# Loading the second batch's first rows between two weight blocks, with 12 stand-in matmuls instead of 16

## The chip, the core and the metric

The kernel runs on one core of one Trainium2 chip. The metric is device time in microseconds (us) of one execution; lower is better. The engines are PE (matmuls, with a separate weight-load track), DVE, ACT and POOL for elementwise work, and SP, which here only issues DMAs. ACT and POOL issue DMAs too.

## What is computed

A global filter along the sequence, then a two-layer network with SiLU on every token:

```python
batch, seq, dim = (8, 3008, 256)          # tokens 8 * 3008 = 24064, d_ff = 2048
X = np.fft.rfft(x, axis=1)
Y = X * (filt_r + 1j * filt_i)[None, :, :]
attn_out = np.fft.irfft(Y, n=x.shape[1], axis=1).astype(np.float32)

h = attn_out.reshape(B * S, D) @ w_in      # (24064, 256) @ (256, 2048)
g = h * (1.0 / (1.0 + np.exp(-h)))
out = (g @ w_out).astype(np.float32)       # (24064, 2048) @ (2048, 256)
```

The weights `w_in` and `w_out` arrive in double precision.

## The kernel before

**The main loop.** The network of all eight batches is a loop of 384 steps (`hidden`, `project`): 48 pairs of token blocks times 8 groups of hidden channels, all matmuls in fp32 (L756 and L819), a Strassen-like scheme with seven products per group. While it runs for batch b, the filter of batch b+1 is worked in between its rounds by a planner (`plan`, `put`), at step and round times written out by hand. That covers nearly all of the time. The instruction order of each engine is the program's order.

**The prologue** is what comes before the loop, some 74 us. It computes the filter of batch 0 alone, converts the first nine weight blocks, and begins batch 1:

- `weights(j)` (L1009, `load_weights` at L904) loads block j of the double-precision weights as two DMAs of 256 KB on SP: 128 columns of w_in (L926) and 128 rows of w_out (L929). Below, w5 stands for block 5, with a first and a second half. `bits`, `converted`, `rounded` and `placed` turn the two 32-bit words of each number into fp32 on DVE and ACT.
- `stage1_first` (L295) is the first transform of batch 0 on PE. It reads x from `w_t`, which is borrowed as a buffer, and from `x_all`.
- `load_filters` (L235) brings the filter on the queues of SP, ACT and POOL; `d_t` and `e_t` are tables of the transforms, loaded by ACT in two parts each (L1069, L1075; L1073, L1076).
- `table` (L1089) makes signed copies of `e_t`; for groups 2 to 5 on ACT (L1095).
- `forward` (L456), `products`, `inverse` (`inverse_first`, L516, and `rows_first`, L531) carry batch 0 through its six groups: matmuls pb (L467) and pc (L527), and between them the multiplication by the filter. `rows_first` copies the result q out of PSUM (L541) and stores it to DRAM (L543): ten of the twelve stores are issued by ACT, each directly behind its copy, and the second ones of groups 4 and 5 by SP.
- `load_t4_rows` (L567) reads those rows back, six DMAs of 256 KB on SP (L571) into a part of `w_t`.
- `second["load_two"]` (L326, through `load_rows`, L275) loads the rows that batch 1's first two stage-1 steps need: one DMA of 768 KB on SP (L277) into `x_all`, called x below. It may not start before `stage1_first` has read batch 0's rows out of `x_all`.
- `second["stage1"]` (L339, L345) transforms them: eight passes on PE. The copies out of PSUM follow on ACT (L361).
- `idle_wide(16)` (L1051, L1055) are stand-ins: matmuls whose result nobody reads, issued by PE between batch 1's stage 1 and the last stage of batch 0. Each is 128x256 and two passes.
- `stage3` (L574, pd, L586) is the last transform of batch 0, and reads the rows that `load_t4_rows` brought. Its copies to y (L600) release the main loop.

SP and ACT issue their DMAs in the program's order. In the prologue SP's order is: w0 to w3, x of batch 0, its share of the filter, a small table (`wi_t`, L1077), w4 to w7, x of batch 1, w8, the two stores of q, the six loads of rows, w9.

Of the kernel before, what the change touches and what calls it, by code (L numbers as in the profile page):

```python
# [170 lines left out]
def kernel(  # L171
# [79 lines left out]
    def bank(b, name, spare=None):  # L251


        if early[0] is None and spare in ("x", "yz"):
            return xps.tile([128, 2, C], FP32, name=name, tag=spare)
        if early[0] is None and spare is not None:
            return accps.tile([128, 2, C], FP32, name=name, tag=f"a{spare}")
        if early[0] is None:
            return fps.tile([128, 2, C], FP32, name=name, tag="f")
        early[0] += 1  # L260
        k = early[0] % 8
        if k < 2:
            return fps.tile([128, 2, C], FP32, name=name, tag="f")
        if k > 5:
            return xps.tile([128, 2, C], FP32, name=name, tag="x" if k == 6 else "yz")
        return accps.tile([128, 2, C], FP32, name=name, tag=f"a{k - 2}")
# [637 lines left out]
    def load_weights(j, queue=None):  # L904

        if j in (8, 11, 12, 13):
            pool, tag = (t4pool, "t4") if j in (11, 12) else (upool, "u")
            raw = pool.tile([128, 2, 512], U32, name=f"raw_{j}", tag=tag)
        else:

            if j in (0, 2):
                t = ypool.tile([128, 2, HALF], FP32, name=f"raw_{j}", tag="y")
                raws.setdefault("tiles", []).append(t)
                raws["at"] = t.rearrange("p a n -> p (a n)").bitcast(U32)[:, 0:2048]
                raws["y"] = raws["at"]
                raws.setdefault("first", raws["at"])
            elif j == 4:
                raws["at"] = spool.tile([128, 2048], U32, name=f"raw_{j}", tag="s")
            elif j == 6:
                raws["at"] = gpool.tile([128, 2048], U32, name=f"raw_{j}", tag="g")  # L920
            elif j in (9, 14):
                raws["at"] = raws["y"]
            at = 1024 * (j in (1, 3, 5, 7, 10, 15))
            raw = raws["at"][:, at:at + 1024].rearrange("p (w n) -> p w n", w=2)
        queue = queue or nc.sync
        queue.dma_start(  # L926
            out=raw[:, 0].rearrange("p (a n) -> p a n", a=2),
            in_=moe_w_in.bitcast(U32)[:, 256 * j:256 * j + 256].rearrange("(a p) n -> p a n", p=128))
        queue.dma_start(out=raw[:, 1], in_=moe_w_out.bitcast(U32)[128 * j:128 * j + 128, :])  # L929
        raws[j] = raw  # L930
# [78 lines left out]
    def weights(*js, queue=None):  # L1009
        for j in js:  # L1010
            if wide:
                load_weights(j, queue)
# [38 lines left out]
    def idle_wide(n, ps=None, rhs=None):  # L1051

        ps = ps or bank(0, "idle")
        for _ in range(n):
            nc.tensor.matmul(out=ps[:, 0], lhsT=wx_t, rhs=wide_rows if rhs is None else rhs,  # L1055
                             start=True, stop=True)
# [18 lines left out]
    nc.scalar.dma_start(out=d_t[:, 16:NS], in_=d_dram[:, 16:NS])  # L1075
    nc.scalar.dma_start(out=e_t[:, 2:NG], in_=e_dram[:, 2:NG])  # L1076
    nc.sync.dma_start(out=wi_t, in_=ws_dram.ap())  # L1077
    weights(4, 5, 6, 7)

    signed = []  # L1080
    for i in range(2):
        t = typool.tile([128, 2, 2, 2, 128], FP32, name=f"signed_{i}", tag="ty")
# [26 lines left out]
    for k in range(16):  # L1109
        part["stage1_first"](k, 2)  # L1110
        if k in whole:
            part["stage1_first"](whole[k], 3)
    second["load_two"]()
    weights(8)
    part["forward"](0, fill=4)
    placed(0, 1)
    for g in range(1, 4):
# [49 lines left out]
    gp.tensor_copy(out=gate, in_=w_t[:, 4, A11, 0, 0:1])  # L1167
    for u in range(2):
        second["store_rows"](u)
    idle_wide(16)  # L1170
    for g in range(4):
        part["stage3"](g)
    nc.sync.dma_start(out=wi_t, in_=wi_dram.ap())
# [93 lines left out]
```

## Time and profile before

Four runs gave 2574.99, 2577.04, 2577.07 and 2578.72 us: median 2577.06. The execution that the profiler recorded took 2574.76 us.

| what | value |
|---|---|
| profiled execution, device time | 2574.76 us |
| its span in the profile | 2572.9 us, 47850 instructions |
| PE busy | 2551.3 us (99%) |
| weight loads (PEld) busy | 2195.7 us (85%) |
| DVE / ACT / POOL busy | 1664.9 / 1091.8 / 430.7 us |
| mean granted clock of PE | 0.996 |
| mean DMA rate | 66 GB/s; 300 and 151 GB/s in the first two of 40 slices |

The span is cut into 40 slices of 64 us for the overview; the prologue is the first slice and a part of the second. There the DMA engines are busy at 90% or more in the first slice and 50% in the second, and in the second slice the granted PE clock is at 0.8 of full speed. In all other slices the clock is at 0.9 or more, and PE is busy for 80% to over 90% of the time.

How the lines are read: a timeline line has its start, its duration, the engine (SPq and ACTq are DMA issues), the line in the kernel, the operation, output<-inputs, and how many are merged; in square brackets stands the engine's idle time ahead of it and what ended that. A matmul in fp32 is recorded as two passes. A DMA in the chain of waits lasts from its issue to its landing.

### The profile page before, as it was taken

To read this page: it belongs to the slowest core of one execution; us is meant where nothing else is said; L and a number is where in the kernel's file an instruction comes from. 1 tells how busy PE (TensorE), PEld (TensorE's weight loads), DVE (VectorE), ACT (ScalarE), POOL (GpSimd) and SP (SyncE) were. 2 spreads that over 40 slices of the span, in tenths; PEclk is the share of its full clock that TensorE was granted. 3 is DMA by queue.
4 is the path that set the end of the run, shared out by engine and by line. 5 is a ranking of instruction groups with operands and counts; after the bars stand their busy time and mean duration, and the time that the engine had idled before them with its cause. 6 is when DMAs were issued, how large, how long until landed. Compare 5 with 4: busy or idle time off the path is not lost.

```text
span 2572.9 us, 47850 instructions
## 1 busy us (share of the span) xinstructions
PE 2551.3 (99%) x18714; PEld 2195.7 (85%) x18714; DVE 1664.9 (65%) x3589; ACT 1091.8 (42%) x3019; POOL 430.7 (17%) x688
## 2 busy tenths in 40 slices
PE   8999999999999999999999999999999999999998
PEld 6688888888888888888888888888888888888987
DVE  7866666676666666666666676666666666555554
ACT  4544444444444444443444344444444444444443
POOL 4212111211121111211121112211121112101101
PEclk9899999999999999999999999999999999999999
DMA  9522232222222222322233122331232211200011
GB/s 300 151 60 55 74 73 64 60 74 66 58 66 66 73 69 48 82 71 66 58 74 77 48 67 63 76 79 46 66 87 66 66 42 33 60 17 16 9 17 16
DMA packets 198554, 171.06 MB, mean 66 GB/s; under 512 B 122068, under 2 KB 173380, under 8 KB 197348
## 3 DMA queue, kind: packets, MB, share of 16 engines
q1 hardware_dynamic: 176056, 117.06, 19.7%
q0 software_dynamic: 17344, 45.70, 5.6%
q10 hardware_dynamic: 4928, 5.24, 0.7%
q8 instruction: 147, 2.41, 0.4%
q14 instruction: 79, 0.65, 0.1%
HBM read 96.07 MB, written 81.26 MB: 69 GB/s over the span
## 4 chain that ended last, share of the span: by engine, by line
PE 96%; DMA 3%; DVE 1%; ACT 0%; issue 0%; ACTq 0%; SPq 0%; DVEq 0%
PE acc L819 44%; PE px L756 26%; PE pyz L756 19%; PE pd L586 3%; PE pb L467 2%; PE pc L510 2%; PE pf L434 1%; DMA w_t<-in_x_dram 0%; PE pa L354 0%; DMA raw<-in_moe_w_out_dram 0%; DMA x_all<-in_x_dram 0%; DMA d<-q 0%; PE pa L345 0%; DMA filt<-in_filt_i_dram 0%; DMA d_t<-d_tbl 0%; DMA w_t<-d 0%
## 5 line engine op out<-in xcount | busy, mean ns | idle before, releaser
L819 PE MATMUL acc<-g,w_t 128*128 128x256 f32 (+1 forms) x5376 | 1508.8, 375 | 0.4 <-DVE g L727 0.4
L819 PEld LDWEIGHTS acc<-g,w_t 128*128 128x128 f32 x5376 | 1021.3, 190 | 115.6 <-DVE g L727 0.8
L727 DVE TENSOR_TENSOR g<-pyz,abc 128x256 f32<-128x256 f32 (+1 forms) x1152 | 480.0, 417 | 619.8 <-ACT abc L777 356.2
L727 DVE TENSOR_TENSOR g<-g 128x256 f32<-128x256 f32 (+3 forms) x1152 | 599.6, 520 | 196.8 <-ACT g L760 183.7
L756 PE MATMUL px<-ty,w_t 128*128 128x256 f32 (+1 forms) x2304 | 678.5, 376 | 1.1 <-ACT abc L771 0.6
L760 ACT ACTIVATE g<-g 128x256 f32<-128x256 f32 (+1 forms) x1152 | 472.9, 410 | 250.2 <-DVE g L727 250.2
L727 POOL TENSOR_TENSOR s<-s 128x256 f32<-128x256 f32 (+1 forms) x329 | 255.2, 793 | 1417.3 <-DVE s L839 1320.8
L756 PEld LDWEIGHTS px<-ty,w_t 128*128 128x128 f32 x2304 | 432.1, 190 | 65.4 <-issue 6.0
L756 PE MATMUL pyz<-y,w_t 128*128 128x256 f32 (+1 forms) x1536 | 453.6, 377 | 0.5 <-DVE g L727 0.4
L756 PEld LDWEIGHTS pyz<-y,w_t 128*128 128x128 f32 x1536 | 283.5, 189 | 48.0 <-DVE g L727 7.9
L771 ACT COPY abc<-px 128x256 f32<-128x256 f32 (+1 forms) x384 | 141.5, 369 | 372.3 <-PE px L756 372.3
L777 ACT COPY abc<-px 128x256 f32<-128x256 f32 (+1 forms) x384 | 141.8, 369 | 338.2 <-PE px L756 337.4
L760 ACT ACTIVATE g<-px 128x256 f32<-128x256 f32 (+1 forms) x384 | 146.1, 380 | 300.0 <-PE px L756 299.9
L756 PE MATMUL px<-y,w_t 128*128 128x256 f32 (+1 forms) x768 | 232.2, 384 | 0.8 <-DVE y L600 0.8
L756 PE MATMUL pyz<-ty,w_t 128*128 128x256 f32 (+1 forms) x768 | 225.8, 376 | 0.3 <-DVE g L727 0.2
L756 PEld LDWEIGHTS px<-y,w_t 128*128 128x128 f32 x768 | 140.3, 189 | 32.7 <-DVE y L606 5.8
L756 PEld LDWEIGHTS pyz<-ty,w_t 128*128 128x128 f32 x768 | 144.6, 190 | 19.1 <-DVE g L727 1.5
L764 ACT COPY abc<-px 128x256 f32<-128x256 f32 (+1 forms) x384 | 135.8, 354 | 52.2 <-PE px L756 52.2
L586 PEld LDWEIGHTS pd<-wi_t,t 48*64 48x64 f32 x3840 | 61.1, 135 | 25.1 <-ACT g L760 16.4
L446 POOL DMA_DIRECT2D d<-tf x144 | 71.9, 506 | 28.8 <-DVE tf L442 28.8
L839 ACT COPY s<-acc 128x512 f32<-128x512 f32 (+1 forms) x94 | 54.3, 578 | 47.5 <-PE acc L819 47.4
L869 DVE STREAM_TRANSPOSE o<-s 128x256 f32<-128x256 f32 x192 | 73.9, 423 | 0.4 <-issue 0.4
(136 smaller groups left out, 1270.7 us busy)
## 6 DMA issues: line engine op xcount, KB each, us to landing
t<-d SPq DMA_DIRECT2D x120, 192.0 KB
t<-d SPq DMA_DIRECT2D x84, 256.0 KB
d<-q POOLq DMA_DIRECT2D x84, 256.0 KB, 2.7
out_dram<-o SPq DMA_DIRECT2D x636, 32.0 KB
d<-tf POOLq DMA_DIRECT2D x144, 96.0 KB, 3.3
xr<-in_x_dram SPq DMA_DIRECT2D x6, 1472.0 KB
x_all<-in_x_dram SPq DMA_DIRECT2D x72, 96.0 KB
x_all<-xr SPq DMA_DIRECT2D x72, 96.0 KB
```

The lines of the kernel that those rows point to most:

```text
L446: nc.gpsimd.dma_start(out=d1[k // 2, :, k % 2, n0:n0 + 4], in_=us["tf"][32 * k:32 * k + NS].rearrange("p q n c -> p (q n) c"))
L467: nc.tensor.matmul(out=ps[k][32 * j:32 * j + 32, ri, :], lhsT=d_t[rows, 4 * g + at, ri, :], rhs=rhs, start=True, stop=True)
L586: nc.tensor.matmul(out=ps[h][c0:c0 + 64, cb, i, :], lhsT=t4[rows, i, 128 * cb + c0:128 * cb + c0 + 64], rhs=wi_t[rows, :], start=True, sto ...
L727: eng.tensor_tensor(out=out, in0=in0, in1=in1, op=op)
L756: nc.tensor.matmul(out=out, lhsT=w_t[:, jp, c, 0], rhs=rhs, start=start, stop=True, skip_group_check=True)
L760: nc.scalar.activation(out=g[:, k, 0:n], in_=g[:, k, 0:n] if src is None else src, func=AFT.Silu)
L764: nc.scalar.copy(out=sums[:, 0, 0:n], in_=xo)
L771: nc.scalar.copy(out=sums[:, 1, 0:n], in_=xo)
L777: nc.scalar.copy(out=sums[:, 2, 0:n], in_=xo)
L819: nc.tensor.matmul(out=acc[pair][i][:, h, 0:n], lhsT=w_t[:, jp, c, 1], rhs=g[:, k, 0:n], start=(jp == 0 and h == 0), stop=last, skip_group ...
L839: copy(out=s[:, 2 * i:2 * i + 2, 0:n], in_=acc[pair][i][:, :, 0:n])
L869: v.transpose(out=o[:, :, h, :], in_=results[pair][:, ((2, 6), (4, 1))[chunk][h], :])
```

## The change

The loads of w5, w6 and w7 are issued behind x of batch 1 instead of ahead of it, and twelve stand-ins run instead of sixteen. The call for w4 moves to just ahead of x in the text.

```diff
@@ -1075,8 +1075,6 @@
     nc.scalar.dma_start(out=d_t[:, 16:NS], in_=d_dram[:, 16:NS])
     nc.scalar.dma_start(out=e_t[:, 2:NG], in_=e_dram[:, 2:NG])
     nc.sync.dma_start(out=wi_t, in_=ws_dram.ap())
-    weights(4, 5, 6, 7)
-
     signed = []
     for i in range(2):
         t = typool.tile([128, 2, 2, 2, 128], FP32, name=f"signed_{i}", tag="ty")
@@ -1110,8 +1108,9 @@
         part["stage1_first"](k, 2)
         if k in whole:
             part["stage1_first"](whole[k], 3)
+    weights(4)
     second["load_two"]()
-    weights(8)
+    weights(5, 6, 7, 8)
     part["forward"](0, fill=4)
     placed(0, 1)
     for g in range(1, 4):
@@ -1167,7 +1166,7 @@
     gp.tensor_copy(out=gate, in_=w_t[:, 4, A11, 0, 0:1])
     for u in range(2):
         second["store_rows"](u)
-    idle_wide(16)
+    idle_wide(12)
     for g in range(4):
         part["stage3"](g)
     nc.sync.dma_start(out=wi_t, in_=wi_dram.ap())
```

## The prediction, made before the changed kernel was run

> **What bounds the kernel now.** I read the engine totals first: PE is busy for 2551.3 of 2572.9 us and the chain of waits is 96% PE. The main loop is matmuls end to end and the change touches none of it. What can move is the stretch ahead of the loop, so I read the chain of waits there. Its columns are start, duration, what ran or was in flight.
>
> ```profile
> 32.94 8.69 DMA raw<-in_moe_w_out_dram
> ...
> 41.71 8.40 DMA x_all<-in_x_dram
> ...
> 50.18 0.37 ACTq L543
> 50.55 0.04 issue
> 50.59 0.60 ACT q L541
> ...
> 51.21 3.61 DMA d<-q
> ...
> 55.54 4.08 DMA d<-q
> ...
> 60.22 6.18 DMA w_t<-d
> 66.41 0.14 issue
> 66.54 7.12 PE pd L586 x254
> ```
>
> The chain says that x of the second batch (41.71) left when weight block 4's second half landed (32.94 + 8.69 = 41.63), and that ACT's sixth store of q (50.18) left when x landed (50.11). Neither needs the other's data. Counting the DMAs that SP and ACT issue, in the order of their issues, x is the eighth after w4's second half, and that store is the eighth after x. So each of these DMAs waits for the one eight places ahead. I use that rule below. From the last store of q (55.54) the chain runs through the load of its rows into w_t to stage 3 (pd) at 66.54.
>
> Then PE's own timeline, and the busy time and clock in five stretches (columns: busy us of PE, weight loads, DVE, ACT, POOL, then granted clock, DMA share, GB/s):
>
> ```profile
> 52.97 3.70 PE L345 MATMUL pa<-x_all,wx_t 96*128 96x512 f32 x8
> 56.50 7.07 PE L1055 MATMUL idle<-d_t,wx_t 96*128 96x256 f32 x32
> 65.56 0.41 PE L586 MATMUL pd<-wi_t,w_t 48*64 48x47 f32 x2 [1.99 <-DMA w_t<-d]
> 66.54 7.07 PE L586 MATMUL pd<-wi_t,w_t 48*64 48x47 f32 x254 [0.56 <-DMA w_t<-d]
> ```
>
> ```profile
> 63.60:65.10 1.50, 0.00 (x0) 0.00 (x0) 1.50 (x3) 1.50 (x4) 0.00 (x0) 1.00 0.71 171
> 65.20:66.50 1.30, 0.41 (x2) 0.28 (x2) 1.26 (x4) 1.27 (x3) 0.00 (x0) 0.50 1.05 255
> 66.60:73.60 7.00, 7.00 (x254) 6.85 (x254) 3.32 (x8) 2.17 (x6) 3.71 (x8) 0.50 0.29 70
> 74.40:78.80 4.40, 3.84 (x8) 2.15 (x8) 3.71 (x10) 1.84 (x5) 0.00 (x0) 0.50 0.85 225
> ```
>
> Three things: the second batch's stage 1 (L345) starts as soon as the matmuls before it are through, with x long landed; the stand-ins (L1055) end at 63.57 and PE then waits 1.99 us for DMA; and the clock is at half from before pd starts until 78.8, although 16 stand-ins ran. Last, the DMA queues (packets, MB, share) in 36 to 40 us, then in 44 to 48 us; q1 is SP's, q10 ACT's:
>
> ```profile
> q10 hardware_dynamic: 274, 0.74, 55.4%
> q1 hardware_dynamic: 630, 0.64, 48.2%
> ...
> q1 hardware_dynamic: 368, 0.98, 102.6%
> ```
>
> **The change, part by part.** **Four stand-ins fewer.** The 32 passes start every 0.216 us (56.5 to 63.2 for 31 intervals), so eight fewer take 8 x 0.216 = 1.73 us less. They end at 61.84 instead of 63.57. What hides this is the wait for w_t<-d: pd's first pass waits until 65.56 whichever number ran. Value 0. A gain of 1.73 us is excluded, since nothing waits for the last stand-in. A loss is possible only by the clock, and in this execution pd ran at half clock anyway, so nothing is left to lose: 0. If some executions keep the full clock through pd now, they would lose the difference: pd's 256 passes took 7.12 us here and 4 x 1.08 = 4.32 in the main loop (64 passes each, at 152.40 and 163.18 in the chain), that is 2.8 us. The upper end is +2.8.
>
> The Trainium skill, "TensorE: Matmul & The Clock Gate", section "Why this matters for your kernels", speaks against this edit: it wants no PE idle gap of more than about 3 us between bursts, or the clock falls back to half. By that rule the gap of 1.99 us should have kept the clock and the new one of 3.7 us would lose it, and the sum would be about 3 us worse; the row has the clock at half after 1.99 us already, and the row decides.
>
> **x moved ahead of w5 to w7.** w4's two DMAs only move in the text: no DMA stands between their old and their new place on SP, so they still leave at 31.07 and 32.94. x takes the place of w5's first half and leaves at 36.72, not 41.71. Its own data wait, for the first batch's stage-1 matmuls that read x_all, was over at 30.7. The six DMAs of w5 to w7 move back by one place: to 37.14, 37.65, 38.13, 40.02, 40.44 and 41.71. w8's first half stays at 42.09. w8's second half now has x eight places ahead and leaves when x lands. The bytes in front of ACT's stores of q are the same 2.8 MB, in another order.
>
> When does x land? In 36 to 40 us SP's queue moved 0.64 MB, of which 0.52 are w4 (512 KB), so what stands behind w4 begins near 39.6 (0.12 MB at some 300 GB/s). x's 768 KB at the 244 GB/s of 44 to 48 us, where x went, take 3.2 us: 42.8, and some 1.5 us to the landing (w4's packets were through near 40, its landing is 41.63): 44.3. w8's second half leaves 1.7 us later than now.
>
> Who is better off: ACT's sixth store. The stores before it come every 1.03 us (46.87, 47.90, 48.92); it should leave at 49.95 and left at 50.18. w7's second half is now eight ahead and stands behind the same bytes as x did, so it lands no later. Gain 0 to 0.23; ACT's chain is what the later pd steps wait for, so I take 0.23.
>
> Who is worse off: e_t's second part (512 KB, ACT's queue, 32.19), which ACT's tables wait for until 41.37; everything after hangs on them. Its last packets went in 36 to 40 us beside SP's, so x may cut in at the very end. Bounds: 0, and +0.6 (one packet of x for each engine: 96 packets over 16 engines in 3.2 us is 0.53 each). Value 0, because x begins when e_t is nearly through.
>
> Behind that stands the queue of stores: the last one took 4.08 us to land, the same stores from POOL 2.7 in the page's DMA list. If the queue empties earlier, up to 1.4 us come out of the chain at 55.54; if w8's late half mixes with the stores, up to +1.0 (one store's spacing). Between -1.4 and +1.0 I take 0: the bytes are the same.
>
> DVE reads w5 at 50.28, w6 and w7 from 55.43, w8 at 56.76; with w4's landing time, 8.69 us, the latest of them, w8's second half, is there at 53.0. These stay hidden, by 3.8 us at least. Without that cover, DVE's conversion would stall by what it is late, and then the `gate` copy on POOL with the stores of t1 behind it. x itself has 8.7 us to spare before 52.97.
>
> **Sum:** 0 - 0.23 + 0 + 0 = -0.2 us against the profiled execution's 2574.76 us (span 2572.9 and 1.9 around it). That execution lies 2.3 below the median of the runs, 2577.06; so the forecast is **2576.8 us, no change**. Its own range: -1.4 below, +0.6 + 1.0 above, and about 1.5 to each side for the spread of the runs (2574.99 to 2578.72): 2574 to 2580. The +2.8 of the clock, alone, ends inside it at 2579.6.
>
> **Rivals.** **A, slower: the wait goes from x to w8's second half.** ACT's eighth store (52.23) now stands behind it, where the queue is in order. It decides if that half lands after 52.0. For it: it leaves late, and 44.3 + 8.69 = 53.0 would already cost 1.0. Against: at 44.3 nothing but w7 and w8 is left in front of it, and the bytes are those that have landed by 52 today. If x lands no earlier than now (50.1; the engines sharing their time over all that is queued), w8's half comes at 50.1 + 3.6 (a store's latency) to 50.1 + 8.69, 53.7 to 58.8, and all of ACT's later stores, and pd, shift by 1.7 to 6.8 us: middle about +4, 2581.
>
> **B, faster: the rows for pd come early enough that the clock is held.** If the store queue drains early (-1.4, -0.23) and pd ran at full clock (-2.8) with the loop's first pairs (1.19 + 0.87 us in the chain, against 0.70 + 0.43 later, -0.9), the sum is -5.3: 2571.8. For it: each piece is a row. Against: PE's gap would still be 65.56 - 1.6 - 61.84 = 2.1 us, no shorter than the one after which the clock fell.
>
> **C, hidden altogether:** x was never waited for by PE, so moving it does nothing, not even 0.23: 2577.1. It isn't told from the forecast by time and shares its chance. That x can't go early, because of its data wait, is excluded by 30.7 against 36.72.
>
> **How the numbers follow.** Forecast with C 0.62, A 0.24, B 0.14. A difference of 0.2%, 5.2 us, is about what a measurement of this kernel can tell from no change. Of A some 0.17 lies beyond it, for what its far end may hold that I can't price (DVE waiting for w8 as well), of B 0.13. So faster 0.13, same 0.62 + 0.07 + 0.01 = 0.70, slower 0.17. The range takes in B's price and most of A: 2571.5 to 2582, leaving out about 0.1 at each end.
>
> **What would show it.** Right: x issued near 36.7; ACT's sixth store near 49.95; stand-ins through 1.7 us sooner and PE idle that much longer ahead of pd; pd near 66.3, at half clock. Wrong: ACT's eighth store waiting for w8 (A); pd's 256 passes in 4.3 us, or starting before 65 (B); ACT's tables starting after 42, which would be e_t pushed back. A difference that begins only in the main loop would refute all of it.

## The result, and the profile after

The changed kernel takes 2581.2 us (median of 35 executions, 2578.07 to 2584.22) against 2577.16 us of the kernel before (53 executions, 2574.33 to 2580.29). The ratio is 1.0016, 95% interval 1.0011 to 1.0021: **slower by 4.0 us, 0.16%**. The forecast was 2576.8 us, 4.4 below; the result lies at the upper end of its range, 2582. By the bound of 0.2% that the prediction took for a measurable difference this would still be no change, but over so many executions the interval excludes 1, and there is a small loss that the forecast had not. The profiled execution took 2580.88 us with a span of 2579.0; beside the one of before that is 6.1 us more.

Where the 6.1 us of this pair lie: the second acc matmul (L819), the end of the prologue, starts at 87.70 us instead of 82.33 (5.4 us), and from there to the 5001st acc matmul it is 2326.16 us instead of 2325.39 (0.8 us). The chain of waits of the changed kernel (start, us, what) no longer goes through x or through ACT's sixth store:

```profile
27.17 6.84 DMA filt<-in_filt_i_dram
...
47.99 10.32 PE pc L527 x64
58.31 1.93 PE pa L345 x4
...
64.07 7.71 DMA w_t<-d
...
71.91 7.12 PE pd L586 x254
```

PE itself is now in it, for 10.32 us of pc. PE's timeline of the same execution says why:

```profile
42.70 1.64 PE L467 MATMUL pb<-w_t,d_t 64*32 64x256 f32 x32
47.99 6.65 PE L527 MATMUL pc<-w_t,signed 64*128 64x256 f32 x31 [3.65 <-POOL z L497]
...
58.24 3.70 PE L345 MATMUL pa<-x_all,wx_t 96*128 96x512 f32 x8
61.78 5.34 PE L1055 MATMUL idle<-d_t,wx_t 96*128 96x256 f32 x24
70.84 0.42 PE L586 MATMUL pd<-wi_t,w_t 48*64 48x47 f32 x2 [3.72 <-DMA w_t<-d]
71.91 7.07 PE L586 MATMUL pd<-wi_t,w_t 48*64 48x47 f32 x254 [0.65 <-DMA w_t<-d]
```

PE stands still for 3.65 us ahead of 47.99 and then needs 6.65 us for 31 passes. In the kernel before it waited 0.28 us there, and 29 passes took 3.50:

```profile
45.87 3.50 PE L527 MATMUL pc<-w_t,signed 64*128 64x256 f32 x29 [0.28 <-ACT q L541]
```

Stage 1 (L345) starts at 58.24 instead of 52.97, the stand-ins are through in 5.34 us instead of 7.07, and the wait ahead of pd is 3.72 us instead of 1.99. The releaser named for the first gap, POOL's z, is not one: that matmul reads w_t and not z. What ended just before is ACT's first copy of q (47.28 + 0.56), which frees a PSUM bank: the kernel takes its eight banks in turn, and these matmuls, of group 2, get the ones that group 0 had. ACT's timeline, first of the changed kernel, then of the kernel before:

```profile
44.44 0.42 ACT L1093 ACTIVATE signed<-e_t 128x256 f32<-128x256 f32 x1 [27.28 <-DMA raw<-in_moe_w_out_dram]
...
47.28 0.56 ACT L541 COPY q<-pc 128x512 f32<-128x512 f32 x1
47.87 0.38 ACTq L543 DMA_DIRECT2D d<-q  x1
```

```profile
41.37 0.42 ACT L1095 ACTIVATE signed<-e_t 128x256 f32<-128x256 f32 x1 [23.30 <-DMA raw<-in_moe_w_out_dram]
...
44.80 0.38 ACTq L543 DMA_DIRECT2D d<-q  x1
```

The tables that ACT makes from e_t (L1095, now L1093) start 3.07 us later, and the first copy and store with them. The packets in the trace show e_t: its second part's 4 KB packets ran from 37.44 to 40.71 us before and run from 37.30 to 43.81 now, while x's 8 KB packets, once at 43.65 to 49.25, run at 37.98 to 43.32, beside them. The DMA queues from 36 to 40 us (packets, MB, share; q1 is SP's, q10 ACT's) say the same in the changed kernel; before, q10 had moved 0.74 MB there:

```profile
q1 hardware_dynamic: 485, 0.98, 79.0%
q10 hardware_dynamic: 109, 0.42, 30.9%
```

Last the granted clock (columns as in the prediction), three stretches of the changed kernel, then one of the kernel before:

```profile
44.00:48.00 4.00, 0.35 (x15) 0.04 (x1) 4.00 (x8) 3.40 (x9) 4.00 (x7) 0.82 1.06 361
48.00:52.00 4.00, 4.00 (x16) 2.99 (x18) 3.23 (x8) 1.82 (x4) 0.60 (x1) 0.50 0.62 209
71.90:78.90 7.00, 6.99 (x254) 6.92 (x254) 1.99 (x5) 2.17 (x5) 4.26 (x9) 0.50 0.39 101
```

```profile
48.00:52.00 4.00, 4.00 (x40) 3.59 (x38) 3.70 (x9) 2.15 (x4) 1.07 (x2) 1.00 1.07 361
```

PE's new gap is followed by a stretch at half clock in pc (48 to 52 us, where the kernel before had 1.00). pd is at half clock in both executions.

### The profile page after: what moved, and what is told of

The parts are those of the page before. It is cut to its first block, busy times and chain, and to the rows that moved or that the text cites. A ratio compares the mean times of both kernels' runs of the same rounds, so it can differ in the third digit from the quotient of the medians.

```text
span 2579.0 us, 47835 instructions
## 1 busy us (share of the span) xinstructions
PE 2551.7 (99%) x18706; PEld 2195.7 (85%) x18706; DVE 1664.8 (65%) x3589; ACT 1090.3 (42%) x3019; POOL 429.7 (17%) x688
## 4 chain that ended last, share of the span: by engine, by line
PE 96%; DMA 2%; DVE 1%; POOL 0%; issue 0%; SPq 0%; ACT 0%; DVEq 0%; ACTq 0%; POOLq 0%
PE acc L819 44%; PE px L756 26%; PE pyz L756 19%; PE pd L586 3%; PE pb L467 2%; PE pc L510 2%; PE pf L434 1%; PE pc L527 1%; DMA w_t<-in_x_dram 0%; PE pa L354 0%; PE pa L345 0%; DMA w_t<-d 0%; DMA filt<-in_filt_i_dram 0%; DMA filt<-in_filt_r_dram 0%; DVE g L727 0%
## 5 line engine op out<-in xcount | busy, mean ns | idle before, releaser
L819 PE MATMUL acc<-g,w_t 128*128 128x256 f32 (+1 forms) x5376 | 1508.7, 375 | 0.4 <-DVE g L727 0.4
L819 PEld LDWEIGHTS acc<-g,w_t 128*128 128x128 f32 x5376 | 1021.3, 190 | 115.6 <-DVE g L727 0.8
L586 PEld LDWEIGHTS pd<-wi_t,t 48*64 48x64 f32 x3840 | 61.3, 135 | 25.9 <-ACT g L760 16.4
```

The costliest lines, as they stand in the source:

```text
L586: nc.tensor.matmul(out=ps[h][c0:c0 + 64, cb, i, :], lhsT=t4[rows, i, 128 * cb + c0:128 * cb + c0 + 64], rhs=wi_t[rows, :], start=True, sto ...
L819: nc.tensor.matmul(out=acc[pair][i][:, h, 0:n], lhsT=w_t[:, jp, c, 1], rhs=g[:, k, 0:n], start=(jp == 0 and h == 0), stop=last, skip_group ...
```

## The experiments

Each kernel of the experiments was timed in 11 executions, beside 21 or 33 of the kernel before; the changed kernel has its 35 beside 53. The difference is that of the means, in us. "Half clock" is the mean time at half clock of the executions, worked out from the granted clock c of each as 2 x (1 - c) x span; c is listed to three digits, a step of 5 us for one execution, so only means of many say something. For the kernel before it is 21.4 to 23.4 in the five sets of executions that stood beside the experiments.

| kernel | x early? | stand-ins | ratio (95%) | difference | half clock |
|---|---|---|---|---|---|
| changed | yes | 12 | 1.0016 (1.0011 to 1.0021) | +4.1 | 26.8 |
| e11, again | yes | 12 | 1.0017 (1.0008 to 1.0026) | +4.3 | 26.7 |
| e1 | yes | 16 | 1.0003 (0.9994 to 1.0012) | +1.1 | 21.1 |
| e12, e1 again | yes | 16 | 1.0004 (0.9995 to 1.0013) | +1.0 | 20.1 |
| e2 | no | 12 | 1.0007 (0.9998 to 1.0015) | +1.5 | 24.4 |
| e8 | no | 4 | 1.0001 (0.9992 to 1.0010) | -0.1 | 27.6 |
| e6 | no | 22 | 1.0002 (0.9993 to 1.0010) | +0.5 | 17.3 |
| e7 | yes | 22 | 1.0010 (1.0001 to 1.0019) | +2.8 | 18.3 |
| e3, tables later | yes | 12 | 1.0017 (1.0008 to 1.0026) | +4.2 | 27.7 |
| e4, tables later | no | 16 | 1.0005 (0.9996 to 1.0014) | +0.9 | 24.4 |
| e5, x behind w5 | half | 12 | 1.0013 (1.0004 to 1.0022) | +3.0 | 24.8 |
| e9, x on POOL | yes | 12 | 1.0014 (1.0005 to 1.0023) | +4.0 | 25.3 |
| e10, x on POOL | no | 16 | 0.9998 (0.9989 to 1.0007) | -0.4 | 20.1 |
| e17, w8 on POOL | yes | 16 | 1.0004 (0.9995 to 1.0013) | +1.4 | 23.9 |
| e13 | yes | 16 short | 1.0013 (1.0004 to 1.0022) | +3.7 | 28.6 |
| e14 | no | 12 long | 1.0007 (0.9998 to 1.0017) | +1.6 | 23.0 |
| e15 | no | 16 long | 0.9995 (0.9986 to 1.0004) | -1.2 | 16.4 |
| e18 | yes | 16 long | 1.0004 (0.9995 to 1.0013) | +0.9 | 16.4 |
| e16, x on POOL | no | 16 long | 0.9996 (0.9987 to 1.0005) | -1.2 | 15.5 |

### One part of the change at a time

e1 is the changed kernel with `idle_wide(16)`, e2 the kernel before with `idle_wide(12)`; e11 and e12 are the changed kernel and e1 once more.

> x moved ahead of w5 to w7, 16 stand-ins kept. Theory (x shares the DMA engines with e_t's second part, which lands 3 us later; ACT's tables, its copies of q and PE follow, and PE's gap there costs it the clock): slower than before by 3 to 5 us, ACT's tables start after 43.5 us, a half-clock interval may begin near 47. Rival 1 (the four stand-ins are what costs): within 1.5 us of before. Rival 2 (ACT's eighth store waits for w8's second half): slower too, but ACT's tables start near 41.4 and the delay first shows at that store.

> Before with 12 stand-ins instead of 16, nothing else. Theory: within 1 us of before, since PE waits for the rows of pd either way and the clock is at half there either way. Rival 1: slower by 2.5 us or more.

> The changed kernel once more, beside the next run on one chip. Both theories: 3 to 5 us above the kernel before (it was 4.0 above it when first timed).

> The changed kernel with 16 stand-ins instead of 12 once more, beside the changed kernel on the same chip. Theory (stand-ins cost nothing, with x early as with x late): within 1.5 us of the changed kernel, so 2 to 4 us above the kernel before, and the 0.7 us measured at first was a low draw. Rival (four stand-ins fewer cost 2 to 3 us only where x goes early, because PE's longer gap then falls on a clock already lost once): at most 1 us above the kernel before, and at least 2 below the changed kernel.

Neither part makes the 4 us. x alone costs 1.1 and, again, 1.0; fewer stand-ins alone cost 1.5. Each of these intervals holds 1. The four kernels with x early and 16 stand-ins of the same or a larger size (e1, e12, e17 and e18 below), 44 executions, are together 1.1 us above the kernel before, about 0.6 to either side. e1's theory of 3 to 5 us fell, and e2's 1.5 lies between what its two sides expected. e12 falls on the side of its rival, so my theory at that point, that stand-ins cost nothing, fell: with x early, 12 instead of 16 cost 3 us. e12's profile shows what x early alone does. ACT's timeline:

```profile
44.31 0.56 ACT L541 COPY q<-pc 128x512 f32<-128x512 f32 x1
47.63 0.38 ACTq L543 DMA_DIRECT2D d<-q  x1
48.05 0.59 ACT L541 COPY q<-pc 128x512 f32<-128x512 f32 x1 [3.18 <-DMA raw<-in_moe_w_in_dram]
```

Here e_t is not late (the copy begins at 44.31, as before), yet the store behind the copy leaves 2.8 us after the copy's end, when a half of w5 has landed. That is the rule of eight places: with x ahead of w5, the DMA eight places ahead of ACT's first store is w5's **first** half, which is now behind x; before, it was w5's second half, with nothing of x ahead of it.

The semaphores in the traces say where this rule comes from. The prologue's DMAs of SP and ACT signal eight semaphores in turn (101, 103 to 107, 109 and 110), and ahead of each stands a wait for its own semaphore, which the DMA eight turns earlier sets when it lands. In the kernel before, x and ACT's sixth store share 103; in the changed kernel w5's first half and ACT's first store share 106. So the rule is one of this program, and not of a queue. It counts turns and not times of issue: e_t's second part has the turn behind w4's second half, though in the kernel before it was issued ahead of it (32.19 and 32.94).

### More and fewer stand-ins

e6 and e8 are the kernel before with 22 and 4, e7 the changed kernel with 22.

> Before with 22 stand-ins instead of 16: they end near 66.0, when the rows for pd land. Theory (the clock falls in PE's gap ahead of pd in a share of the executions, the more often the longer the gap): the clock is held into pd, pd takes 4.3 to 5.7 us instead of 7.1 and the kernel is 1 to 4 us faster than before, with more of the full clock granted. If the gap plays no part: within 1 us, or slower by up to 0.6 for stand-ins that end after the rows have landed.

> The changed kernel with 22 stand-ins instead of 12. Theory: the loss ahead of pd is gone, x's delay is left: 1 to 3 us faster than the changed kernel by its runs (2581.2), that is 1 to 3 us slower than before, and 1 to 3 us slower than the kernel before with 22 stand-ins. If x's delay is the whole loss: still 4 us slower than before.

> Before with 4 stand-ins: PE idles for 7 us ahead of pd instead of 2. Theory (once the gap is long enough the clock always falls before pd, and a longer gap costs nothing more): as with 12, 0.5 to 3 us slower than before. If each stand-in has its price: 4 us or more slower.

The half-clock time follows the stand-ins' length (27.6 us with 4, 17.3 with 22), but the time does not follow the half-clock time: 22 gain nothing, where 1 to 4 us were expected. e7 came out as expected, 1.3 us below the changed kernel. The next heading but one finds out why. e8 never fitted: by the price found there, its 6 us more at half clock should have cost 1.5 us, and it lost nothing.

### x early: the order, or the bytes?

e3 and e4 move ACT's tables behind `inverse(0)`, in the changed kernel and in the one before, so that the first store doesn't depend on e_t. e5 puts x one block later. e9 and e10 take x off SP's order.

```diff
# e3 on the changed kernel, e4 on the kernel before
+    inverse(0)
     for g in range(2, NG):
         table(nc.scalar, g)
-    inverse(0)
# e5, on the changed kernel
-    weights(4)
+    weights(4, 5)
     second["load_two"]()
-    weights(5, 6, 7, 8)
+    weights(6, 7, 8)
# e9, on the changed kernel (load_two hands the queue on to load_rows); e10 has this line behind inverse(0) of the kernel before
-    second["load_two"]()
+    second["load_two"](nc.gpsimd)
# e17, on e1
-    weights(5, 6, 7, 8)
+    weights(5, 6, 7)
...
     inverse(0)
+    weights(8, queue=nc.gpsimd)
```

> The changed kernel with ACT's four tables moved behind the copies and stores of group 0's q, so that these no longer stand behind the wait for e_t. Theory: ACT's first copy of q comes near 39 to 40 instead of 47.3, the banks come free, and most of the loss is gone: between -2 and +2 us against before. Rival 2 (store waiting for w8) and any theory in which x costs by its bytes ahead of the stores: still +3 to +5 us.

> Before with the same move of ACT's tables. Theory: two copies with their stores (2.05 us) come out of the chain behind e_t, so pd starts 1 to 2 us earlier: faster than before by 1 to 2 us. If ACT's chain did not set pd's start, no change.

> The changed kernel with x one weight block later: w4 and w5 ahead of it, w6 to w8 behind it; 12 stand-ins. Theory (x's packets beside e_t's are what delays ACT's tables): w5 fills that time instead, the tables start within 0.7 us of before, and only the price of the 12 stand-ins is left: 0.5 to 2.5 us slower than before. If it is x's place ahead of w6 to w8, or any early place of it: still 3 to 5 us slower.

The first stores' waits show plainly in ACT's timeline: of e3, of e4, and of e5:

```profile
48.27 0.38 ACTq L543 DMA_DIRECT2D d<-q  x1
48.70 0.58 ACT L541 COPY q<-pc 128x512 f32<-128x512 f32 x1 [9.78 <-DMA raw<-in_moe_w_in_dram]
```

```profile
42.90 0.38 ACTq L543 DMA_DIRECT2D d<-q  x1
43.32 0.59 ACT L541 COPY q<-pc 128x512 f32<-128x512 f32 x1 [4.38 <-DMA raw<-in_moe_w_out_dram]
```

```profile
49.14 0.58 ACT L541 COPY q<-pc 128x512 f32<-128x512 f32 x1 [2.77 <-DMA x_all<-in_x_dram]
```

In e3 and e4 the copy itself came at 38.34 and 38.35. Its store left at 48.27 with x early and at 42.90 with x late: 5.4 us for the same store, behind weights it has nothing to do with. In e5 the eighth DMA ahead of the second store is x itself. None of the three did what my theories expected: e3 kept the whole loss (+4.2), e4 gained nothing (+0.9; its tables came at 44.35, behind the held stores, and not at 41.37), and e5, whose tables started at 41.31 as expected, lost 3.0. So the order does hold stores back. But it isn't needed for the loss:

> The changed kernel, but x of the second batch is loaded on POOL's queue instead of SP's, at the same early place; 12 stand-ins. It then stands in no one's way in the order of SP's and ACT's DMAs: w5 to w8 keep their old order among themselves. Theory (the loss comes from x standing in SP's order, so that ACT's first stores of q wait for halves of w5 that moved behind it): the first store leaves at 44 to 46 us, not 47.9, pd starts near 68 and the time is 0 to 1.5 us above the kernel before. Rival (the loss comes from the bytes of x in the air beside the second part of e_t, whichever queue they are on): ACT's tables start after 42.5, pd near 70 to 72, and the time is 2.5 to 4 us above the kernel before, as in the changed kernel.

> The kernel before, with x of the second batch loaded on POOL's queue behind the fourth-order tables' inverse instead of on SP's behind w7; 16 stand-ins. ACT's sixth store then no longer waits for x, and w8 has x neither ahead of it nor in its order. Theory (order decides): the sixth store leaves one spacing (1.0 us) behind the fifth, the last load of t4 rows leaves 0.2 to 1 us earlier, and the time is 0 to 1.5 us below the kernel before. Rival (x's bytes beside the stores cost what the wait cost, or the time hangs on something behind pd): within 0.5 us of the kernel before or above it.

> x early on SP as in the changed kernel, 16 stand-ins, and w8's two halves on POOL's queue behind the tables' first inverse. That takes two DMAs out of the order of SP and ACT: ACT's first store then has e_t's second part eight places ahead and not w5's first half, which the third store gets. Theory (what x early costs ahead of the loop is the wait of the first stores for the halves of w5): the first store leaves right behind its copy, before 46, PE's gap between 44 and 48 us is under 1.5 us in all, and the time is within 0.6 us of the kernel before. Rival (the bytes of x beside e_t's second part and the weights cost it, whatever stands eight places ahead): 1 us or more above the kernel before, as with x early and 16 stand-ins.

e9 leaves the order of w5 to w8 as it was and is still 4.0 us slower (its 12 stand-ins are part of that); the tables started at 41.85 and the first store, held by a half of w5, left at 45.92, so its store kept to the theory and its time to the rival. e10's -0.4 fits both of its sides. e17 takes the wait away: nothing stands between copy and store any more. But in that execution e_t was late, as in the changed kernel, and PE's gap was 4.02 us (ACT's line, then PE's):

```profile
44.61 0.42 ACT L1093 ACTIVATE signed<-e_t 128x256 f32<-128x256 f32 x1 [27.52 <-DMA e_t<-e_tbl]
...
48.04 0.38 ACTq L543 DMA_DIRECT2D d<-q  x1
```

```profile
48.15 2.17 PE L527 MATMUL pc<-w_t,signed 64*128 64x256 f32 x6 [4.02 <-ACT q L541]
```

Its time, +1.4, is that of e1 and e12. That is the rival's outcome: **768 KB of x ahead of ACT's chain cost it, by whichever of the two transfers behind them is late in an execution**, e_t's second part or w5's first half. In the profiles with x early the first store leaves at 45.4 to 49.6 us, with x late at 43.6 to 45.9, e4 left aside. e_t's packets took 6.5 us in the changed kernel's profile and 5.6 in e17's, where x's began within 1.4 us of them; in the other eighteen profiles they took 2.1 to 4.0. In each of the other nine profiles with x early the first store waited behind its copy, for 0.3 to 9.4 us (2.6 in e11, the changed kernel again); with x late it left 0.03 us behind it, e4 left aside. How the loss divides between the two stays open.

### The stand-ins: their time, or their number?

From the second acc matmul to the 5001st, ten profiles with 16 stand-ins take 2325.4 us on average, seven with 12 take 2326.8, two with 22 take 2327.4, and one with 4 takes 2325.2. The difference is in runs of 128 pd passes in the main loop. With 12, the two runs near 654 and 2234 us take 6.0 us together on average; in each profile with 16 they take 4.7. That is the whole of the 1.3 us. With 22 the runs near 670 and 1296 us take 3.1 to 3.3 us each instead of 2.1. Most of it is single gaps of PE in the middle of a run. PE's timeline of e2 (12), e10 (16) and e6 (22):

```profile
2231.17 2.06 PE L586 MATMUL pd<-wi_t,t 48*64 48x47 f32 x123 [0.26 <-DVE g L727]
2233.94 0.32 PE L586 MATMUL pd<-wi_t,t 48*64 48x47 f32 x3 [0.71 <-issue]
```

```profile
2227.26 2.07 PE L586 MATMUL pd<-wi_t,t 48*64 48x47 f32 x126 [0.26 <-DVE g L727]
```

```profile
1292.65 2.08 PE L586 MATMUL pd<-wi_t,t 48*64 48x47 f32 x126
1295.70 0.26 PE L586 MATMUL pd<-wi_t,t 48*64 48x47 f32 x2 [0.96 <-issue]
```

Nothing that the profile shows ended those waits. In five of the seven profiles with 12 the gap comes three or four passes before the end of the run near 2234 us, in two (the changed kernel and e5) in the run near 654 us, and in both profiles with 22 near 670 and 1296 us. So 8 of 9 profiles with 12 or 22 have a gap of more than 0.3 us, and none of the eleven with 16 or 4 has one. The DMA queues of e2 from 2230.7 to 2233.0 us name a suspect:

```profile
q8 instruction: 1, 0.02, 2.4%
```

A queue of kind "instruction" brings 16 KB packets, 147 in all in the kernel before, whose PE has some 37,600 records: about 256 instructions to a packet. A run of pd is 128 passes with 128 weight loads, 256 instructions in 2.1 us, the densest of the program. In e2 such a packet began 0.74 us after the run did (2231.34 and 2230.60), and the gap ended 2.60 us after the packet's start. Over the eleven gaps of more than 0.3 us this is 2.2 to 2.9 us, longer than the 2.1 us in which PE uses up a packet's worth. In e10 the packet began 3.1 us ahead of the run. Four stand-ins are 16 PE instructions, so they shift all that follows against those packets. That PE waited for the packet is argued from these times; no record names it. The Trainium skill, "Runtime: NRT & Kernel Launch", section "Instruction fetch mechanics", says that instructions are streamed in 16 KiB blocks of 256 and that crossing into the next is mostly hidden; the packets agree, and in these runs of pd it was not hidden.

So the next kernels hold the number or the time of the stand-ins and change the other:

```diff
# e13, on the changed kernel: columns n = 192, idle_wide(16)
# e14, on the kernel before: n = 340, idle_wide(12)
# e15, on the kernel before: n = 352, idle_wide(16); e16, the same on e10
# e18, on the changed kernel: n = 352, idle_wide(16)
-            nc.tensor.matmul(out=ps[:, 0], lhsT=wx_t, rhs=wide_rows if rhs is None else rhs,
+            nc.tensor.matmul(out=ps.rearrange("p a c -> p (a c)")[:, 0:n], lhsT=wx_t,
+                             rhs=d_t[0:96].rearrange("p s r n -> p (s r n)")[:, 0:n],
```

> The changed kernel with 16 stand-ins of 192 columns instead of 12 of 256: the same time on PE (16 x 192 = 12 x 256 columns), but PE's stream of instructions as long as in the kernel before. Theory (four stand-ins fewer shift PE's program against the 16 KB blocks in which it is loaded, and a block then comes late in a dense run of pd passes in the main loop; x early costs 1 to 2.5 us ahead of the loop): no PE gap over 0.3 us in the main loop, second acc to the 5001st in 2325.4 us and not 2326.9, and the time 1 to 2.5 us above the kernel before. Rival (the shorter stand-ins cost by their time, through the clock): 3.5 to 4.5 us above the kernel before, like the changed kernel.

> The kernel before with 12 stand-ins of 340 columns instead of 16 of 256: the same time on PE, but PE's stream as short as in the changed kernel; x stays late. Theory (program position): a PE gap of 0.7 to 1.1 us in a run of pd passes near 2230 us or near 655 us, second acc to the 5001st in 2326 to 2327.5 us, and the time 1 to 2 us above the kernel before. Rival (time of the stand-ins): no gap, within 0.5 us of the kernel before.

> The kernel before with its 16 stand-ins at 352 columns each, so they last as long as 22 and PE's stream keeps its length. Theory (the run with 22 stand-ins held the clock ahead of the loop and gave the gain back in two gaps of 1 us in the loop, by its program position): pd at full clock, at most 7 us at half clock before the second acc, no gap in the loop, and the time 1 to 2 us below the kernel before. Rival (the clock ahead of the loop is worth nothing): within 0.5 us of the kernel before, as with 22.

e13's profile has no gap in the loop and 2324.9 us for it, as the theory had it, but its time is the rival's, +3.7: its mean of 28.6 us at half clock is the highest of all. e14's profile has no gap over 0.3 us, but it lost time in the same two runs of pd as the others with 12. PE's timeline of e14, then of the kernel before:

```profile
645.26 2.07 PE L586 MATMUL pd<-wi_t,t 48*64 48x47 f32 x125
647.51 0.32 PE L586 MATMUL pd<-wi_t,t 48*64 48x47 f32 x3 [0.19 <-issue]
...
2227.66 2.34 PE L586 MATMUL pd<-wi_t,t 48*64 48x47 f32 x126 [0.26 <-DVE g L727]
```

```profile
646.37 2.08 PE L586 MATMUL pd<-wi_t,t 48*64 48x47 f32 x128
...
2228.15 2.07 PE L586 MATMUL pd<-wi_t,t 48*64 48x47 f32 x126 [0.26 <-DVE g L727]
```

A packet of instructions began with each of the two runs (645.28 and 2227.07), and the loop takes 2326.2 us. So all seven profiles with 12 stand-ins have one of these runs longer or both, and none of the ten with 16, whatever the stand-ins' size. e14's time, +1.6, is the theory's, but its executions go from 2574.5 to 2583.1 and its interval holds 1. e15 lies 1.2 us below the kernel before by the means, as expected; its interval holds 1 too. Its profile missed the full clock that was expected: pd's rows came later than the end of the long stand-ins, and the clock was at half for 20.5 us from 66.9 on.

```profile
66.96 0.42 PE L586 MATMUL pd<-wi_t,w_t 48*64 48x47 f32 x2 [2.03 <-DMA w_t<-d]
67.98 7.07 PE L586 MATMUL pd<-wi_t,w_t 48*64 48x47 f32 x254 [0.60 <-DMA w_t<-d]
```

These three asked for the clock's price. Within each kernel, over the 351 executions of the experiments, slower ones are those with more half-clock time: 0.24 us for each us (correlation 0.68). This alone doesn't say which is the cause, since a late chain also makes PE's gaps longer. With that as a third term:

> The changed kernel with 16 stand-ins of 352 columns instead of 12 of 256; x stays early. New theory, three terms: over all runs so far a kernel's executions cost 0.24 us for each us that PE spends at half clock (12 short stand-ins: 5 us more of it than before, 1.1 to 1.3 us of time); 12 instead of 16 stand-ins put about 1.4 us of waits into the main loop by the length of PE's program; x early costs 1.5 us by itself. This kernel keeps only the third and has less half-clock time than the kernel before (some 17 us against 22, 1.2 us): 0 to 1 us above the kernel before, 3 to 4 below the changed kernel. Rival (x early alone makes the 4 us): 3 us or more above the kernel before.

> The kernel before with its 16 stand-ins at 352 columns each, so they last as long as 22 and PE's program keeps its length, and with x of the second batch on POOL's queue behind the tables' first inverse. By the three terms: half-clock time of 16 to 18 us instead of 22, worth 1 to 1.4 us; x on POOL 0 to 0.4; so 1 to 2 us below the kernel before. Rival (half-clock time only goes along with slow executions and isn't their cause): within 0.5 us of the kernel before.

e18 keeps x early and undoes the rest: +0.9, where the changed kernel has +4.1. e16 came out at -1.2. Both are as the three terms have it. A least-squares fit to all 19 rows of the table (e5 counted as early) gives 1.8 us for x early, 1.5 for 12 stand-ins instead of 16, 1.3 for 22, and 0.16 us for each us of half clock, with about 0.4, 0.5, 0.8 and 0.06 to either side. The rows lie within 1.1 us of it, e8 the farthest. PE's timeline of e16, then of e13, around pd:

```profile
56.02 9.63 PE L1055 MATMUL idle<-d_t,wx_t 96*128 96x352 f32 x32
65.58 0.31 PE L586 MATMUL pd<-wi_t,w_t 48*64 48x47 f32 x2
66.44 3.78 PE L586 MATMUL pd<-wi_t,w_t 48*64 48x47 f32 x242 [0.55 <-DMA w_t<-d]
71.20 0.43 PE L586 MATMUL pd<-wi_t,w_t 48*64 48x47 f32 x12 [0.98 <-issue]
```

```profile
60.97 5.36 PE L1055 MATMUL idle<-d_t,wx_t 96*128 96x192 f32 x32
70.06 0.28 PE L586 MATMUL pd<-wi_t,w_t 48*64 48x47 f32 x2 [3.73 <-DMA w_t<-d]
71.12 7.07 PE L586 MATMUL pd<-wi_t,w_t 48*64 48x47 f32 x254 [0.78 <-DMA w_t<-d]
```

With long stand-ins PE has only short gaps here (0.55 us) and pd runs at full clock, from 66.44 to 71.63, even with a gap of 0.98 us of the "issue" kind in it; with short ones it waits 3.73 us and pd takes 7.07 at half clock. e15's profile above shows that long ones do not ensure it in every execution. Long stand-ins with x late are the best version found: e15 and e16 together, 22 executions, are 1.2 us below the kernel before, about 0.9 to either side, while each alone has an interval that holds 1. Against the changed kernel they gain some 5 us.

## Why the prediction was wrong, step by step

**The sum.** It had 0 - 0.23 + 0 + 0. By the runs, the changed kernel's +4.1 us can be divided into three terms, each about 1 us uncertain: x early, 1.1 and 1.0 with 16 stand-ins (e1, e12; 1.5 when their shorter half-clock time is put back); more half-clock time, 26.8 us instead of some 22.3 at 0.24 us each, 1.1; and the gaps in the loop, 1.3 us by the profiles' means (2326.8 against 2325.4). Together 3.9. The fit to the timed executions alone divides it much alike: 1.8, 0.7 and 1.5, together 4.0. The first rests on kernels that differ from the kernel before in nothing else (e1, e12), the third on the profiles and the fit. The price of the half clock is a correlation, which e15 and e16 bear out and e8 does not. The third fits e6 against e15 (same stand-in time, 22 against 16 of them: 1.7 us apart) and not e13 alone.

**"Four stand-ins fewer. Value 0": failed.** The cover named, the wait for w_t<-d, was there, and pd waited for its rows in both profiles. The reason for 0, "in this execution pd ran at half clock anyway, so nothing is left to lose", took one execution for all. Executions differ in their half-clock time, and the stand-ins' length moves the mean: 15 to 18 us with the time of 22 of them, 20 to 24 with that of 16, 24 to 29 with less. The prediction's own upper bound, +2.8, holds the 1.1. The Trainium skill's rule on idle gaps ("TensorE: Matmul & The Clock Gate", "Why this matters for your kernels"), which the prediction set aside for that one row, pointed the right way: e16 without a long gap had pd at full clock, e13 with 3.73 us at half. Its bound of about 3 us isn't sharp here: the row of before lost the clock after 1.99 us, and that of e15 after 2.03.

**"The main loop ... the change touches none of it": failed**, and no bound covered it. What PE runs in the loop is the same, but it starts 16 instructions sooner in the program. The prediction wrote that a difference beginning only in the main loop would refute all of it; 0.8 of the 6.1 us of the profiled pair do.

**"x moved ahead of w5 to w7": the step that failed ahead of the loop.** The rule of eight places was right in effect (e3, e4, e5; by the times of issue, which the prediction counted, x is the seventh after w4's second half, by the semaphores' turns the eighth), and it was applied to ACT's sixth and eighth stores only. The sixth is better off, as predicted: it now follows the fifth by 1.03 us, and by 1.26 before. The first store's place eight ahead, a half of w5, was not looked up: w5 "stays hidden" was argued from DVE's reads alone. And **e_t**, "value 0, because x begins when e_t is nearly through": x left SP at 33.60, not 36.72, its packets began at 37.98, not 39.6, and the last packet of e_t moved by 3.1 us where the upper bound was 0.6. That bound allowed each DMA engine one packet of x; x's 96 packets of 8 KB ran beside nearly all of e_t's 128 of 4 KB. "ACT's tables starting after 42", named as the sign, came at 44.44, and pd at 71.91 instead of 66.3. That e_t was so late is one draw: in e11, the same kernel, its last packet came at 41.91, and the first store then waited 2.6 us for w5.

**The rivals.** A had the right kind, a wait of ACT's stores behind weights that x pushed back, and its price of +4 was met by accident: it put it at the eighth store and w8, where nothing was late. That the range holds the result is owed to this price, so it is luck too. B's mechanism, a held clock, exists (e15, e16), for 1.2 us and not 5.3, and not by this change. C was refuted by e1 and e12 only weakly (+1.1 and +1.0, each interval holding 1) and by PE's new gap plainly.

## What to carry to other kernels

When a DMA is moved forward, list every later DMA and instruction, on every queue, that gets a new predecessor on its semaphore (here the one eight places ahead) or shares the engines with its packets, and look at the earliest first: here the first store mattered, not the sixth. Price a clock effect over many executions, since one profile shows one draw. And when matmuls are added or taken out ahead of a long unrolled loop, compare the loop itself too: fill by size (wider stand-ins) changes the time without shifting the program, fill by number does both.

## What was not expected of the hardware

- Runs of small matmuls can outrun the loading of PE's instructions: gaps of up to 1.06 us in runs of 128 pd passes, which came with 16 PE instructions fewer or 24 more at a place 590 to 2170 us earlier. Why a packet comes 3 us ahead of a run in one kernel and within it in another is open.
- A transfer can be stretched by one that starts just behind it on another queue: e_t's 512 KB in 4 KB packets took 3.3 us before and 6.5 with x's 8 KB packets beginning 0.7 us behind them (5.6 at 1.4 us in e17). With x's beginning some 2 us behind or later, still early, it was 3.1 to 4.0. Whether the packets' size matters was not tried.
- Profiled executions showed the effect of x larger than the runs do: with x early their spans are 4.9 us longer on average than with x late (11 and 9 profiles), the means of the timed executions of the same kernels only 2.6. Each profile is one execution, so this may be chance. The profiles were used for places, the runs for sizes.
